# Norm weights multiplied into transposed q in place, and due times of single operations found by annealing, in an attention and feed-forward kernel on one core

## Chip, cores, metric

One core of one Trainium2 chip. The metric is the time of one execution on the device in microseconds (us), lower is better; medians over several executions.

## The reference, cut

Attention over q, k, v of shape (8, 12, 448, 64) with an RMS norm on q and k, then a feed-forward layer on the 3584 tokens of 768.

```python
def rmsnorm(x, g):
    return x / np.sqrt(np.mean(x * x, axis=-1, keepdims=True) + 1e-06) * g
q_n, k_n = rmsnorm(q, g_q), rmsnorm(k, g_k)
attn = softmax(q_n @ k_n.T / 8) @ v            # per batch and head
x = attn.transpose(0, 2, 1, 3).reshape(3584, 768)
h = x @ w_in                                    # 768 -> 2048
sp = np.maximum(h, 0.0) + np.log1p(np.exp(-np.abs(h)))
return (h * erf(sp)) @ w_out                    # 2048 -> 768
```

A "pair" below is two heads of one batch element; there are 48.

## The kernel before

The kernel adds some 3950 operations to a plan. Each has an engine (P TensorE, V VectorE, A ScalarE, G GpSimd, S SyncE), a cost in us and a due time. A list scheduler inside the kernel then walks through time and gives each free engine the ready operation with the earliest due time; what comes out is the order in which the instructions are emitted, so each engine runs them in that order on the chip. The plan also models a port that VectorE and GpSimd share: an operation marked `port` that finds the lock taken is lengthened until the lock's end.

```python
# Plan.order(), the part that starts an operation
took = o.cost if type(o.cost) is float else o.cost[e]
if e in "VG" and o.port:
    took += max(0.0, lock - now - 0.13)
    lock = now + took
free[e] = now + took
...
PAIR, BATCH, N_PE, N_COL = 8.59, 54.26, 8, 6
W_IN, W_OUT, W_RATE = 2, 9, 4
FILL, FILL_SHARE, MERGED, TWO_GROUPS = 1.98, 0.73, 1, 1
```

For a pair transposed by DMA, three GpSimd multiplications write a scaled copy of k (both norm weights in one vector `gcomb`) into one of two kp buffers, on a zero background, so that the third block of keys can be two full matmuls:

```python
for i, (r, c0, s0, w, c) in enumerate(((0, 0, S + D, JS, 0.75), (0, JS, S, D, 0.14), (D, S, S, S, 0.86))):
    ...
            nc.gpsimd.tensor_tensor(dst, src, g.to_broadcast((D, w)), op=ALU.mult)     # kp <- qT * gcomb
    add(engs, ..., t0 - 3, scaled, reads=["gcomb", ("qT", m), ("kp0", kp)], writes=[("kp", kp, i)], port=True)
```

The w_in loads are paced, one after each of the pairs 2 to 5:

```python
if 0 <= n - W_IN < NC:
    load = add_w_in(n - W_IN, [load, ends[-1]])
```

The softmax here doesn't subtract the row's maximum and nothing guards it: scores larger than these inputs give would overflow.

## Time and profile before

| | before |
|---|---|
| time, median of 3 | 475.87 us (475.81 to 478.84) |
| span of the profiled run | 473.3 us |
| busy: TensorE, VectorE, ScalarE, GpSimd | 448.1, 326.7, 376.1, 285.6 us |
| lost TensorE time 10 to 60, 60 to 180, 180 to end | 17.3, 15.5, 2.5 us |
| TensorE's own work | 424.0 us |

"Lost" is read as the prediction does: from the start of each matmul to the start of the next, less 189, 162.5 or 56 ns by its kind, where more than 0.11 us is left, and the whole of each idle product. (The prediction gives 2.7 us from 180 us on and 3.3 after the last matmul; counted again in the same way for all kernels, these are 2.5 and 3.7.) "Own work" is the span less what was lost, the time before the first matmul and the time after the last. All such figures, and the lags below, come from the one execution of each kernel that was profiled; executions of one kernel lie 1 to 7 us apart, so differences of 2 us or less between two of them say little. Three stages of the kernel before, by window (window and width, then busy us and instructions of PE, PEld, DVE, ACT, POOL, then clock, DMA share, GB/s):

```profile
100.00:120.00 20.00, 18.75 (x102) 8.71 (x100) 17.79 (x23) 15.05 (x24) 14.57 (x20) 1.00 0.55 93
180.00:240.00 60.00, 59.83 (x339) 30.57 (x338) 46.43 (x67) 52.91 (x72) 46.38 (x62) 1.00 0.59 144
300.00:320.00 20.00, 19.63 (x113) 10.80 (x111) 14.82 (x23) 19.26 (x20) 5.86 (x6) 1.00 0.28 86
```

After 180 us TensorE is all but full in every stage.

### The profile page before, as it was taken

To read this page: it belongs to the slowest core of one execution; us is meant where nothing else is said; L and a number is where in the kernel's file an instruction comes from. 1 tells how busy PE (TensorE), PEld (TensorE's weight loads), DVE (VectorE), ACT (ScalarE), POOL (GpSimd) and SP (SyncE) were. 2 spreads that over 40 slices of the span, in tenths; PEclk is the share of its full clock that TensorE was granted. 3 is DMA by queue.
4 is the path that set the end of the run, shared out by engine and by line. 5 is a ranking of instruction groups with operands and counts; after the bars stand their busy time and mean duration, and the time that the engine had idled before them with its cause. 6 is when DMAs were issued, how large, how long until landed. Compare 5 with 4: busy or idle time off the path is not lost.

```text
span 473.3 us, 7387 instructions
## 1 busy us (share of the span) xinstructions
PE 448.1 (95%) x2556; PEld 227.4 (48%) x2556; DVE 326.7 (69%) x460; ACT 376.1 (79%) x495; POOL 285.6 (60%) x393
## 2 busy tenths in 40 slices
PE   7768999899898999999999999999999999999997
PEld 3333344444344445554455445554455445655664
DVE  2986677698875997499866975598665933285811
ACT  3587887997789988997889988998889987996500
POOL 6898898858894599828992589619980560000000
PEclk9799999999999999999999999999999999999999
DMA  8929999875977056912793168704942111110221
GB/s 184 276 65 222 192 240 224 136 165 82 229 187 171 19 140 162 231 50 58 169 235 108 21 165 187 198 34 98 221 90 83 21 36 35 66 36 7 78 82 69
DMA packets 108646, 60.00 MB, mean 127 GB/s; under 512 B 59456, under 2 KB 108608, under 8 KB 108608
## 3 DMA queue, kind: packets, MB, share of 16 engines
q1 hardware_dynamic: 101824, 52.64, 46.3%
q0 software_dynamic: 5440, 6.29, 8.7%
q10 hardware_dynamic: 1344, 0.59, 0.5%
q8 instruction: 20, 0.33, 0.3%
q14 instruction: 18, 0.15, 0.1%
HBM read 45.61 MB, written 11.01 MB: 120 GB/s over the span
## 4 chain that ended last, share of the span: by engine, by line
PE 62%; POOL 14%; DVE 9%; ACT 6%; issue 5%; DMA 3%; SPq 1%; POOLq 0%; DVEq 0%; ACTq 0%
PE f L586 25%; PE f L536 21%; PE o L479 11%; POOL sq L265 5%; PE s L454 4%; POOL kp L305 3%; PE s L442 3%; DVE qk L283 2%; POOL qk L283 2%; DVE h L320 2%; POOL vx L413 2%; DMA sp<-in_k_dram 2%; ACT sp L554 1%; ACT sp L550 1%; POOL vm L408 1%
## 5 line engine op out<-in xcount | busy, mean ns | idle before, releaser
L536 PE MATMUL f<-xT,w_in_sb 128*128 128x448 bf16 x768 | 163.6, 353 | 4.9 <-DVE h L320 3.3
L460 ACT ACTIVATE e<-s 128x896 bf16<-128x896 f32 x144 | 126.3, 915 | 4.0 <-PE s L454 2.4
L305 POOL TENSOR_TENSOR kp<-qT,gcomb 64x384 bf16<-64x384 bf16 (+2 forms) x120 | 90.6, 761 | 61.6 <-PE s L454 57.0
L536 PEld LDWEIGHTS <-w_in_sb 128*128 128x128 bf16 x768 | 73.1, 98 | 81.2 <-issue 17.0
L320 DVE COPY h<-f 128x448 f32<-128x448 f32 x105 | 64.9, 620 | 31.3 <-PE f L536 30.2
L265 POOL TENSOR_TENSOR sq<-raw 128x896 f32<-128x896 f32 x42 | 72.6, 1729 | 18.7 <-DVE st L267 9.2
L479 PE MATMUL o<-e,vm 128*128 128x448 bf16 (+1 forms) x324 | 74.1, 360 | 3.7 <-DVE xT L501 1.4
L586 PE MATMUL f<-w_out_sb,g 128*128 128x384 bf16 x384 | 67.4, 326 | 0.8 <-DVE ob L320 0.8
L320 DVE COPY ob<-f 128x384 f32<-128x384 f32 x52 | 28.8, 556 | 55.3 <-PE f L586 54.0
L586 PE MATMUL f<-w_out_sb,godd 128*128 128x384 bf16 x384 | 65.1, 326 | 0.0
L267 DVE TENSOR_REDUCE st<-sq 128x14 f32<-128x896 f32 x42 | 45.5, 1084 | 20.1 <-POOL sq L265 19.5
L550 ACT ACTIVATE sp<-h 128x1792 f32<-128x1792 f32 x31 | 50.4, 1686 | 3.6 <-DVE h L320 3.5
L554 ACT ACTIVATE sp<-sp 128x1792 f32<-128x1792 f32 x32 | 52.6, 1690 | 0.1
L586 PEld LDWEIGHTS <-g 128*128 128x128 bf16 x384 | 37.0, 98 | 29.2 <-issue 4.6
L495 ACT ACTIVATE r<-o 64x448 f32<-64x448 f32 x42 | 22.7, 541 | 34.3 <-PE o L479 34.1
L586 PEld LDWEIGHTS <-godd 128*128 128x128 bf16 x384 | 37.3, 98 | 25.9 <-issue 1.1
L283 POOL TENSOR_TENSOR qk<-raw,st 128x512 bf16<-128x512 f32 x42 | 46.9, 1122 | 1.6 <-ACT st L272 0.3
L283 DVE TENSOR_TENSOR qk<-raw,st 128x384 bf16<-128x384 f32 x42 | 42.4, 1029 | 4.2 <-ACT st L272 2.6
L479 PEld LDWEIGHTS <-vm 128*128 128x128 bf16 (+1 forms) x324 | 28.0, 101 | 30.8 <-issue 8.5
L454 PE MATMUL s<-qT,kp 128*128 128x448 bf16 x120 | 35.7, 352 | 1.6 <-ACT e L460 1.5
L413 POOL CAST vx<-vs 64x64 bf16<-64x64 f32 x96 | 30.0, 314 | 7.1 <-PE o L479 2.7
L501 DVE TENSOR_TENSOR xT<-o,r 64x448 bf16<-64x448 f32 x42 | 25.7, 611 | 12.5 <-ACT r L499 12.0
(71 smaller groups left out, 483.3 us busy)
## 6 DMA issues: line engine op xcount, KB each, us to landing
vl<-in_v_dram SPq DMA_DIRECT2D x48, 192.0 KB, 3.6
out_dram<-ob SPq DMA_DIRECT2D x48, 192.0 KB, 1.9
raw<-in_q_dram SPq DMA_DIRECT2D x21, 384.0 KB, 4.4
raw<-in_k_dram SPq DMA_DIRECT2D x21, 384.0 KB, 4.9
w_in_sb<-in_moe_w_in_dram POOLq DMA_DIRECT2D x4, 768.0 KB, 9.2
w_out_sb<-in_moe_w_out_dram POOLq DMA_DIRECT2D x8, 384.0 KB, 5.1
vs<-in_v_dram SPq DMA_DIRECT2D x16, 96.0 KB, 4.9
out_dram<-ob SPq DMA_DIRECT2D x16, 96.0 KB, 2.2
```

What stands on the lines that cost most here:

```text
L265: add("G", 1.72, tg, lambda part=part: nc.gpsimd.tensor_tensor(sq, part, part, op=ALU.mult), reads=ks, writes=["sq"], port=True)
L267: add("V", 1.08, tg, lambda ss=ss, x=x: nc.vector.tensor_reduce(ss[:, 14 * x : 14 * x + 14], sq, axis=AX.X, op=ALU.add), reads=["sq"], wri ...
L283: add(eng, cost, tg - 27.29, lambda e=e, g=g: e.tensor_tensor(qks[qi].rearrange("p g h d -> p h g d")[:, :, g], raw[:, :, g], w[:, :, g, N ...
L305: nc.gpsimd.tensor_tensor(dst, src, g.to_broadcast((D, w)), op=ALU.mult)
L320: nc.vector.tensor_copy(dst, src)
L454: add("P", cost, t0 + s - 2.54, lambda dst=dst, lhs=lhs, rhs=rhs: nc.tensor.matmul(dst, lhs, rhs, start=True, stop=True), reads=[("qT", m) ...
L460: add("A", 0.918, t0 + s + 1.84, lambda e=e, st=st: nc.scalar.activation(e, st[:, :, :S], func=FN.Exp), reads=[("s", sl, 0), ("s", sl, 1), ...
L479: add("P", cost, t0 + s + 2.3, lambda s=s, dst=dst, lhs=lhs, rhs=rhs: nc.tensor.matmul(dst, lhs, rhs, start=(s == 0), stop=(s == 3)), read ...
L536: add("P", 0.1887, 1e4 + BATCH * (b + 1) + f, lambda f=f, kt=kt, fp=fp: nc.tensor.matmul(fp[:, :S], w_in_sb[:, kt, f * P : (f + 1) * P], x ...
L550: add("A", 1.665 + (1.283 if c == order[0] else 0), -1e3, lambda c=c, h=h: nc.scalar.activation(sps[c], h, func=FN.Softplus), reads=[("h", ...
L554: add("A", 1.665 + (1.283 if c == order[0] else 0), -1e3, lambda c=c: nc.scalar.activation(sps[c], sps[c], func=FN.Erf), writes=[("sp", c, ...
L586: add("P", 0.1617, 1e4 + BATCH * (b + 2.88) + ti, lambda src=src, col=col, nt=nt, js=js, fp=fp: nc.tensor.matmul(fp[:, :JS], src[nt // 4][ ...
```

## The change

Its intent: less work on GpSimd (one in-place multiplication of q by the norm weights and two small copies per pair, instead of three multiplications into kp), a start retuned with due times by batch, and a shorter plan, by due times of single operations found by annealing.

```diff
-    SEM = 0.08
+    SEM = 0.09
+DUES = {
+    0: -18.703, 1: -60.012, 2: -60.006, 4: -60.009, 5: 15.776, 6: -16.681, ...    # 1148 entries, cut
+}
-    N_VL, N_E, N_EM, N_R, N_X, N_H, N_O = 2, 4, 2, 2, 2, 5, 2
+    N_VL, N_E, N_EM, N_R, N_X, N_H, N_O = 2, 6, 2, 2, 2, 5, 2
-    kps = ring(sb, N_KP, [P, 7 * P], BF16, "kp")
+    kps = ring(sb, N_KP, [P, P], BF16, "kp")
-    PAIR, BATCH, N_PE, N_COL = 8.59, 54.26, 8, 6
-    W_IN, W_OUT, W_RATE = 2, 9, 4
+    PAIR, BATCH, N_PE, N_COL = 8.31, 54.15, 9, 6
+    W_IN, W_STEP, W_OUT, W_RATE = 1, 0, 7, 2
+    DUE = dict(...)                       # due offsets per kind and batch, cut
+    FILL, FILL_SHARE, MERGED = 1.19, 0.45, 1
-        for i, (r, c0, s0, w, c) in enumerate(...):       # three scaled copies into kp
+        def gained():
+            ...
+                nc.gpsimd.tensor_tensor(qT[:, :S], qT[:, :S], gcomb.to_broadcast((P, S)), op=ALU.mult)
+        add("G", {"G": 0.86, "V": 0.32}, t0 - DUE['sc'][b], gained, reads=["gcomb", ("qT", m)], writes=[("qTg", m)], port=True)
+        for i in range(2):
+            ...copied: kp[r, r] <- qT[r, S : S + D]
-                if split:
+                if split or s == 2:       # the third block is a pair of 64-row matmuls
-            if 0 <= n - W_IN < NC:
-                load = add_w_in(n - W_IN, [load, ends[-1]])
+            for c in range(NC):
+                if n == W_IN + c * W_STEP:
+                    load = add_w_in(c, [load, ends[-1]] if W_STEP or not c else [load])
+    for i, due in DUES.items():
+        plan.ops[i].due = due
     order = plan.order()
```

Also cut: row-tail loads in three pairs of transfers, copies out of PSUM on two engines in the first pair, the last block's copies in halves.

## The prediction

> **What bounds the kernel now.** I read the busy row of the page, its forty slices, the end of the chain, the stage table, the waits and the costliest groups, in that order.
>
> ```profile
> PE 448.1 (95%) x2556; PEld 227.4 (48%) x2556; DVE 326.7 (69%) x460; ACT 376.1 (79%) x495; POOL 285.6 (60%) x393
> ...
> PE   7768999899898999999999999999999999999997
> ...
> POOL 6898898858894599828992589619980560000000
> PEclk9799999999999999999999999999999999999999
> ```
>
> TensorE is the bound: 95% busy, at full clock apart from the first slices. Only the first third of the span has digits under 9 (and the last slice). But busy time flatters it, since a matmul's recorded span reaches into the next one. The rate at which matmuls really follow one another is in the last lines of the chain, in order of time (start us, us, what):
>
> ```profile
> 415.36 18.17 PE f L536 x96
> 433.53 36.41 PE f L586 x224
> 469.97 0.56 DVE ob L320
> ```
>
> 18.17/96 = 189 ns per 448-column matmul and 36.41/224 = 162.5 ns per 384-column one, though their rows give 353 and 326 ns. So I took the start of every matmul in the trace, subtracted these intervals (56 ns for the 128-column transposes), and call the rest above 0.11 us per gap, plus the idle products on the zero tile (189 ns each), lost:
>
> - 0 to 10.3 us: before the first real matmul, all lost.
> - 10 to 60 us: gaps 15.8 us, idle products 1.5: 17.3 us.
> - 60 to 180 us: gaps 10.8 us, 25 idle products 4.7: 15.5 us.
> - 180 to 470 us: 2.7 us in 290.
> - After the last matmul: 3.3 us.
>
> That is 49 us; 424 us of the 473 is matmul work at its own pace. The change can win only where time is lost. The stage table agrees (window, width, then busy us and instructions of PE, PEld, DVE, ACT, POOL, clock, DMA):
>
> ```profile
> 20.00:30.00 10.00, 8.13 (x66) 3.78 (x62) 7.59 (x12) 8.36 (x14) 9.62 (x11) 0.92 0.56 138
> 30.00:40.00 10.00, 7.53 (x71) 4.22 (x69) 9.37 (x11) 8.26 (x15) 9.53 (x9) 1.00 0.70 122
> 40.00:50.00 10.00, 7.59 (x55) 2.77 (x51) 4.32 (x9) 7.81 (x15) 7.83 (x14) 1.00 1.10 227
> ...
> 120.00:140.00 20.00, 17.13 (x99) 8.48 (x98) 15.56 (x16) 17.22 (x30) 19.12 (x27) 1.00 0.94 208
> 140.00:160.00 20.00, 18.40 (x100) 9.76 (x100) 14.65 (x23) 19.06 (x16) 8.86 (x9) 1.00 0.50 119
> ...
> 240.00:260.00 20.00, 20.00 (x118) 11.00 (x117) 13.30 (x20) 18.36 (x18) 11.44 (x12) 1.00 0.55 152
> ```
>
> From 20 to 40 us GpSimd is 95% busy, and in 120 to 140, where TensorE idles most after the start, 96%. The chain restricted to 115 to 150 us gives lines of GpSimd about 43% of that stretch. What GpSimd does (group line: busy us, mean ns; wait line: us in total, times, longest):
>
> ```profile
> L305 POOL TENSOR_TENSOR kp<-qT,gcomb 64x448 bf16<-64x448 bf16 x40 | 38.5, 962 | 2.7
> L305 POOL TENSOR_TENSOR kp<-qT,gcomb 64x384 bf16<-64x384 bf16 x40 | 35.0, 875 | 56.6 <-PE s L454 55.3 <-DMA qT<-qk 0.6
> L413 POOL CAST vx<-vs 64x64 bf16<-64x64 f32 x96 | 30.0, 314 | 7.1 <-PE o L479 2.7 <-DMA vs<-in_v_dram 1.5
> L305 POOL TENSOR_TENSOR kp<-qT,gcomb 64x64 bf16<-64x64 bf16 x40 | 17.8, 444 | 2.3 <-PE s L454 1.7
> ```
>
> ```profile
> POOL kp L305 <- PE s L454: 57.0, 10, 17.6
> ```
>
> Three multiplications per pair write a scaled copy of k into one of only two buffers, so GpSimd also stands 57 us waiting for score matmuls to free one. Most of that is late, where it costs nothing: the waits of 20 to 180 us hold 8.0 of it, in two pieces, one of 7.0 us.
>
> **What the Trainium skill says.** "Perfetto Trace Analysis", section "Identifying the Most-Contended Engine", says that matmul busy share does not show distance from the roofline; the trace agrees (353 ns recorded, 189 ns apart). "TensorEngine Tiling (Array Packing)", "Key Properties": changing the tiling mode drains TensorE. The trace agrees: near 190 us a group of two 64-row pairs has start-to-start times 285, 3, 197, 3, 282 ns, 0.58 us where two full matmuls would take 0.38. "GPSIMD Engine Reference", "4.1 Engine selection", says that two-input operations are about twice as slow there and one-input ones nearly line-rate; here the 64-column multiplication took 444 ns and the 64-column cast 314. "TensorE: Matmul & The Clock Gate", "What's actually happening", has the clock halved after an idle window of about 3.4 us; the trace has two such stretches, 11.3 to 14.7 and 18.1 to 21.5 us.
>
> **The change, part by part.**
>
> Norm weights. Per DMA-transposed pair, 0.962 + 0.875 + 0.444 = 2.28 us on GpSimd become one in-place multiplication of 128x448 and two 64x64 copies. The L305 rows give (962 - 875)/64 = 1.36 ns per column with no sign that partitions matter, so the multiplication should take about 0.96 us and the copies 0.31 as the casts: 1.59 us. The build has 39 such pairs (one more is transposed on TensorE): 40 x 2.28 - 39 x 1.59 = 29 us less on GpSimd, 286 to about 257. The path from the landed transpose to the first scores shrinks from three operations to one, 1.3 us, and the wait for a free kp goes, as the result stays in the four qT buffers.
>
> Scores. The third block can no longer be two full matmuls on zero-padded k; it becomes a 64-row pair. Alone that costs one entry and one exit: 285 + 3 + 282 - 189 = 381 ns, against 2 x 189 = 378. The build has 115 entries into 64-row mode against 64, yet nearly the same price: 39 x 0.003 us, plus a split pair and seven more transposes for the ninth TensorE-transposed pair, about +0.7 us in all.
>
> Start. The row-tail loads become three pairs of transfers instead of two, so pair 1 doesn't wait for 160 KB (now until 10.5 us); the first pair's two copies out of PSUM go to two engines at once instead of 0.38 + 0.44 us in line; six e buffers instead of four let the exponentials run ahead; all w_in loads follow pair 1. In the trace the first five attention results leave at 22.1, 27.8, 33.7, 38.5 and 42.6 us, 5.1 us apart, and the first projection matmul starts at 43.2. ScalarE needs 3 x 0.915 + 0.547 + 0.538 + 0.576 = 4.4 us per pair. At 4.5 us apart the fifth comes 2.5 us sooner; with some of the gaps up to 60 us closed as well I take 17.3 down to 12.5: -4.8.
>
> Order of single operations. The annealed due times move nearly everything between 40 and 180 us. The build holds 10 + 3 + 2 idle products in three places after the start, where before there were 25 in one; with the new share of 0.45 that is 15 x 0.19/0.45, about 6 us of gaps the schedule itself still expects, against 25 x 0.19/0.73 = 6.5. Unforeseen ones come on top (4 us seems fair, where about 9 of the 15.5 were unforeseen before), minus what less GpSimd work absorbs: 15.5 to 9: -6.5.
>
> After 180 us: 2.7 to 2.5, -0.2. End: the last block is copied by two engines in halves and stored from two queues, 0.56 us to about 0.33, and smaller stores: -0.5.
>
> Sum: -4.8 - 6.5 - 0.2 - 0.5 + 0.7 = -11.3, so 475.9 - 11.3 = 464.6 us; call it 464.5.
>
> **Rivals.** (1) GpSimd was never the cause: the gaps early on are a lack of matmul work, set by ScalarE's 4.4 us per pair and three table loads per batch. For it: ScalarE is 86 to 95% busy from 120 to 160, and DVE close behind. Against: GpSimd is busier in just the window with the longest gap. Then relief moves the wait to ScalarE and half of the middle gain goes: about 470. (2) Over-fitted order: each engine takes its instructions strictly in the planned order, so an order tight on paper loses when a load lands late; DMA already runs at a share above 1 in the stages 40 to 80 us, and all w_in loads now fall earlier. Against: from 180 us on the old plan lost 2.7 us in 290, so plans of this kind do hold. It would leave 468 to 474. (3) Everything closes, 10 to 180 us losing only about 12 of 33: about 455. (4) The mode changes cost more than the 3 ns when the pairs stand between other matmuls: 50 x 0.1 = +5 us, about 469.
>
> **Range and chances.** The threshold for 2% is 466.4, only 1.9 us above my number. Recovering a third of the 33 us lost between 10 and 180 gives 464; a quarter gives 467; half gives 459. As the change aims its whole effort at this loss I think better than a third somewhat likelier than worse: faster 0.61, same 0.37, slower 0.02; range 456.5 to 471.
>
> **What would show it.** Right: GpSimd busy near 257 us with the in-place row at 39 x about 0.96; no wait of GpSimd for score matmuls worth naming; the first projection matmul near 40.5 us; lost time about 12.5 in 10 to 60 and 9 in 60 to 180; TensorE's intervals still 189 and 162.5; span near 462. Wrong: the in-place row far above 1 us, gaps above 15 us again in 60 to 180 with ScalarE or DVE as releaser, a first projection matmul not before 43, or added time above 2 us at the 64-row pairs.

## The result

The changed kernel is slower: 491.25 us median of 4 runs (490.02 to 492.36) against 476.58 us for the kernel before on the same chip (475.81 to 478.84, 4 runs). The ratio is 1.0299, 95% interval 1.0254 to 1.0344. Here and below a ratio is the mean time of one kernel's fast runs over that of the other's of the same rounds, so not quite the ratio of the medians quoted. The output is correct.

The page of the changed kernel, busy row and TensorE's two rows of the forty slices:

```profile
PE 457.8 (93%) x2560; PEld 222.2 (45%) x2560; DVE 324.1 (66%) x463; ACT 379.2 (77%) x495; POOL 255.6 (52%) x388
...
PE   8488999878989999999999997999999999999996
...
PEclk9987999998989999999999999999999999999999
```

TensorE is busy for 10 us more and yet a smaller share of the span. In the row of before all slices from 160 us to the last but one were nines; here a 7 stands in the slice at 294 to 306 us. The clock row dips at four slices up to 150 us, where before it dipped at one. The stages from 20 to 50 us, and those of the table above:

```profile
20.00:30.00 10.00, 6.22 (x46) 2.73 (x44) 7.97 (x8) 5.95 (x12) 5.30 (x6) 0.83 0.49 122
30.00:40.00 10.00, 8.00 (x63) 3.36 (x61) 7.46 (x9) 8.68 (x17) 7.08 (x11) 1.00 0.78 148
40.00:50.00 10.00, 8.84 (x51) 3.26 (x51) 6.70 (x11) 6.36 (x12) 8.35 (x11) 0.66 0.74 152
100.00:120.00 20.00, 15.39 (x73) 6.33 (x72) 18.02 (x23) 13.91 (x19) 13.08 (x18) 0.91 0.53 94
180.00:240.00 60.00, 55.94 (x311) 26.93 (x310) 38.40 (x58) 50.76 (x68) 38.76 (x56) 1.00 0.57 141
300.00:320.00 20.00, 16.89 (x103) 9.47 (x101) 12.39 (x16) 14.78 (x14) 10.57 (x12) 1.00 0.54 138
```

Against the rows of before: 20 to 30 us fell from 8.13 to 6.22 busy us, 100 to 120 from 18.75 to 15.39, 180 to 240 from 59.83 to 55.94 and 300 to 320 from 19.63 to 16.89. From 30 to 50 us it is busier than before (8.00 for 7.53, 8.84 for 7.59), but at a clock of 0.66 in the second of these stages, where before it was 1.00. The span grew by 17.3 us, and the parts of the prediction's own table add up to that:

| us | before | predicted | after | change |
|---|---|---|---|---|
| before the first matmul | 10.3 | 10.3 | 10.6 | +0.3 |
| lost 10 to 60 | 17.3 | 12.5 | 20.3 | +3.0 |
| lost 60 to 180 | 15.5 | 9.0 | 17.9 | +2.4 |
| lost 180 to the last matmul | 2.5 | 2.5 | 10.0 | +7.5 |
| after the last matmul | 3.7 | 3.2 (-0.5) | 4.0 | +0.3 |
| TensorE's own work | 424.0 | 424.7 | 427.7 | +3.7 |

What the change does to GpSimd came out as intended. Groups (line, engine, operation, out<-in, count, busy us, mean ns, idle us before it and its releaser):

```profile
L499 POOL COPY kp<-qT 64x64 bf16<-64x64 bf16 x78 | 25.9, 333 | 54.1 <-PE s L664 51.1
...
L489 POOL TENSOR_TENSOR qT<-qT,gcomb 128x448 bf16<-128x448 bf16 x39 | 36.2, 930 | 19.1 <-DMA qT<-qk 18.7
```

The waits (engine, tile and line, what it waited for: us in total, times, longest):

```profile
POOL kp L499 <- PE s L664: 51.1, 8, 17.2
...
PE f L749 <- DVE h L513: 7.2, 5, 3.9
...
PE f L524 <- DVE g L582: 3.4, 1, 3.4
...
PE f L799 <- DMA w_out_sb<-in_moe_w_out_dram: 1.7, 1, 1.7
```

The in-place multiplication takes 930 ns, and GpSimd is busy 255.6 us. But its long wait for score matmuls did not go; it moved from the multiplications to the small copies. The other three lines are waits of TensorE. The longest, 3.9 us before 112 us, is for a VectorE copy behind a run of multiplications, the first of them at 102 us and over three times as long as the shortest of its line. The last is for a w_out load that had not landed, at 138 us. In between, the transposes wait, once and for 3.4 us, for a VectorE multiplication. That wait is read closely in the timeline (start us, us, engine, line, operation, out<-in, count, idle us before it and releaser):

```profile
18.23 0.95 POOL L604 CAST vm<-vl 128x384 bf16<-128x384 f32 x2
...
18.53 5.88 DVE L582 TENSOR_TENSOR g<-sp,s 128x896 bf16<-128x896 f32 x2 [0.64 <-DMA raw<-in_k_dram]
...
19.14 3.31 POOL L571 TENSOR_TENSOR sp<-sp 128x896 f32<-128x896 f32 x2
...
23.46 0.34 PE L524 MATMUL f<-ident,g 128*128 128x128 bf16 x3 [3.44 <-DVE g L582]
```

Two VectorE multiplications took 5.88 us, the first of them 4.88 where the shortest of that line takes 1.07. Meanwhile GpSimd ran four operations one after another, two casts and two multiplications, and TensorE stood 3.44 us until the product came. The same pattern at 301 us:

```profile
300.75 1.04 POOL L472 TENSOR_TENSOR qk<-raw,st 128x512 bf16<-128x512 f32 x1
...
301.17 3.68 DVE L472 TENSOR_TENSOR qk<-raw,st 128x384 bf16<-128x384 f32 x1
...
301.75 1.67 POOL L454 TENSOR_TENSOR sq<-raw 128x896 f32<-128x896 f32 x1
...
303.39 1.04 POOL L472 TENSOR_TENSOR qk<-raw,st 128x512 bf16<-128x512 f32 x1
...
305.43 0.73 PE L692 MATMUL o<-e,vm 128*128 128x448 bf16 x3 [2.46 <-DVE xT L714]
```

One VectorE multiplication (0.54 us at its shortest) took 3.68 us, beside three GpSimd operations without a gap between them; the VectorE operation that TensorE needed (xT, L714) came after it, and TensorE stood 2.46 us. In both cases the VectorE operation has two inputs in SBUF. Here the Trainium skill's page "SBUF — State Buffer", section "SBUF: two separate sides", bears on the case: VectorE with two SBUF inputs and GpSimd share a port pair as an exclusive lock, and the one that starts first has it for its whole instruction. The trace agrees that VectorE is held, but not that it is held for one instruction: it was passed over at the end of one GpSimd operation, and again at the next.

The kernel before has such cases too, this one at 124 us, in the stage whose idle TensorE the prediction put down to GpSimd's load:

```profile
123.83 2.03 POOL L305 TENSOR_TENSOR kp<-qT,gcomb 64x448 bf16<-64x448 bf16 x2
123.95 4.33 DVE L283 TENSOR_TENSOR qk<-raw,st 128x384 bf16<-128x384 f32 x2
...
125.83 2.04 POOL L283 TENSOR_TENSOR qk<-raw,st 128x512 bf16<-128x512 f32 x2
...
128.99 0.35 PE L479 MATMUL o<-e,vm 128*128 128x448 bf16 x1 [0.77 <-DVE xT L501]
```

Two VectorE multiplications took 4.33 us, the second of them 3.18, and soon after TensorE waited 0.77 us for a VectorE product that came behind it. Summed over the span, two-input VectorE operations lasted 31 us longer than the shortest of their line in the kernel before and 26 us in the changed one. So the holds did not become more. That each of them costs more in the changed kernel is what the experiments below test.

How it costs can be seen from the plan, since the kernel computes a start time for every operation. Take the real start of a matmul less its planned start as the lag. The old plan is 474.3 us long, and its last matmul starts 3.8 us earlier than planned: an early lag of 1.6 us is recovered. The new plan is 470.6 us long, 3.7 us shorter, and its lag climbs: +3.7 us after the held product at 19 us, +5.4 by 41 us, +8.5 after 112 us (another VectorE multiplication held 3.25 us at 102 us), +11.5 by 184, +16.4 after the one at 301 us, +16.7 at the end. Twice some of it is given back (from +6.7 to +3.1 between 97 and 106 us, from +11.3 to +9.3 between 155 and 163), and both times it is lost again within some 20 us; after 184 us no dip is over 1.2 us.

### The profile page after: what moved, and what is told of

The parts are those of the page before. It is cut to its first block, busy times and chain, and to the rows that moved or that the text cites. A ratio compares the mean times of both kernels' runs of the same rounds, so it can differ in the third digit from the quotient of the medians.

```text
span 490.6 us, 7353 instructions
## 1 busy us (share of the span) xinstructions
PE 457.8 (93%) x2560; PEld 222.2 (45%) x2560; DVE 324.1 (66%) x463; ACT 379.2 (77%) x495; POOL 255.6 (52%) x388
## 4 chain that ended last, share of the span: by engine, by line
PE 70%; DVE 8%; DMA 8%; POOL 5%; ACT 5%; issue 2%; SPq 1%; POOLq 0%; DVEq 0%
PE f L799 25%; PE f L749 24%; PE o L692 13%; PE s L664 5%; PE s L630 3%; DVE g L779 2%; DMA qT<-qk 2%; DVE qk L472 2%; DMA w_out_sb<-in_moe_w_out_dram 1%; DMA vl<-in_v_dram 1%; ACT sp L763 1%; POOL kp L499 1%; DMA sp<-in_q_dram 1%; ACT sp L767 1%; POOL sq L454 1%
## 5 line engine op out<-in xcount | busy, mean ns | idle before, releaser
L749 PE MATMUL f<-xT,w_in_sb 128*128 128x448 bf16 x768 | 166.6, 355 | 8.0 <-DVE h L513 7.2
L671 ACT ACTIVATE e<-s 128x896 bf16<-128x896 f32 x144 | 126.3, 915 | 17.7 <-PE s L664 10.7
L513 DVE COPY h<-f 128x448 f32<-128x448 f32 x116 | 71.2, 620 | 41.7 <-PE f L749 40.6
L692 PE MATMUL o<-e,vm 128*128 128x448 bf16 (+1 forms) x324 | 79.7, 366 | 4.5 <-DVE xT L714 2.5
L513 DVE COPY ob<-f 128x384 f32<-128x384 f32 x45 | 24.8, 555 | 54.3 <-PE f L799 50.3
L499 POOL COPY kp<-qT 64x64 bf16<-64x64 bf16 x78 | 25.9, 333 | 54.1 <-PE s L664 51.1
L472 POOL TENSOR_TENSOR qk<-raw,st 128x512 bf16<-128x512 f32 x42 | 49.4, 1179 | 8.2 <-ACT st L461 5.7
L489 POOL TENSOR_TENSOR qT<-qT,gcomb 128x448 bf16<-128x448 bf16 x39 | 36.2, 930 | 19.1 <-DMA qT<-qk 18.7
L472 DVE TENSOR_TENSOR qk<-raw,st 128x384 bf16<-128x384 f32 x42 | 35.7, 864 | 5.2 <-ACT st L461 2.7
L692 PE MATMUL o<-em,vx 128*128 128x448 bf16 (+1 forms) x108 | 34.0, 374 | 0.0
L664 PE MATMUL s<-qT 64*128 64x448 bf16 (+1 forms) x150 | 29.6, 376 | 3.7 <-ACT e L671 1.5
```

Of the source, the lines that this page charges most:

```text
L472: add(eng, cost, tg - DUE['nq'][b], lambda e=e, g=g: e.tensor_tensor(qks[qi].rearrange("p g h d -> p h g d")[:, :, g], raw[:, :, g], w[:, ...
L489: nc.gpsimd.tensor_tensor(qT[:, :S], qT[:, :S], gcomb.to_broadcast((P, S)), op=ALU.mult)
L513: nc.vector.tensor_copy(dst, src)
L664: add("P", cost, t0 + s - DUE['s'][b], lambda dst=dst, lhs=lhs, rhs=rhs: nc.tensor.matmul(dst, lhs, rhs, start=True, stop=True), reads=[(" ...
L671: add("A", 0.918, t0 + s + DUE['ae'][b], lambda e=e, st=st: nc.scalar.activation(e, st[:, :, :S], func=FN.Exp), reads=[("s", sl, 0), ("s", ...
L692: add("P", cost, t0 + s + DUE['aa'][b], lambda s=s, dst=dst, lhs=lhs, rhs=rhs: nc.tensor.matmul(dst, lhs, rhs, start=(s == 0), stop=(s == 3)),
```

## The experiments

Theory: the annealed order is too tight. It assumes that VectorE waits for one GpSimd operation and that loads land as planned; where that fails, the delay is on the path and stays. Rivals: the in-place multiplication itself or its 64-row pairs cost the time; the retuned parameters do; or the lower clock (17.1 us at half clock against 6.8) is a cause of its own. "The time before" in each case is that of the runs beside it, 476.9 to 478.2 us.

### The table of due times taken out

```diff
-    for i, due in DUES.items():
-        plan.ops[i].due = due
```

> The changed kernel without the annealed due times of single operations; everything else of the change stays. Theory A (the annealed order has no slack, so that each late operation delays all that follows): most of the 15 us goes, 475 to 481 us, and lost TensorE time after the start falls from 49 us to 33 or less. Theory B (the in-place weights and their 64-row pairs cost it): stays at 487 us or more. Between, both have a share.

Measured: 484.45 us, ratio 1.0142 (1.0105 to 1.0178). The lag of the end is +1.9 us. Its plan is 6.7 us longer than the one with the table, yet it is about 7 us faster. So the table itself makes about half of the loss, and the rest of the change makes the other half; the time lies between the two theories' ranges, as "both have a share" has it.

### The in-place multiplication alone, on the kernel before

```diff
-    three scaled copies into kp (448, 384 and 64 columns), due t0 - 3        # abridged
+    nc.gpsimd.tensor_tensor(qT[:, :S], qT[:, :S], gcomb.to_broadcast((P, S)), op=ALU.mult)
+    two copies kp[r, r] <- qT[r, S : S + D]; all three due t0 - 20.53
-                if split:
+                if split or s == 2:
```

The due times are the old ones but for these three operations: they have the changed kernel's, 17.5 us ahead of the old.

> The kernel before with the norm weights in place alone (one multiplication, two 64x64 copies, third score block as a 64-row pair), its old due times and parameters. Theory B: 485 us or more. Theory A: within 1% of 476.6, 474 to 481; TensorE's own work up by 1 to 3 us for 40 more entries into 64-row mode, GpSimd busy 27 us less.

Measured: 480.64 us, ratio 1.0072 (1.0036 to 1.0108). The busy row of its page, and its wait for score matmuls:

```profile
PE 449.8 (95%) x2560; PEld 220.8 (46%) x2560; DVE 314.1 (66%) x456; ACT 377.6 (79%) x499; POOL 254.2 (53%) x391
```

```profile
POOL kp L308 <- PE s L455: 63.1, 14, 17.1
```

GpSimd fell from 285.6 to 254.2 us, and TensorE's busy time rose by 1.7 us. Lost time is 18.2 us in 10 to 60, 15.5 in 60 to 180 and 4.5 after that, against 17.3, 15.5 and 2.5 before (the profiled execution is the fastest of this kernel, 477.97 us). Taking 31 us of work off GpSimd closed none of the gaps. But the relief did not reach the stages in which the prediction found GpSimd full, as the stage table of this run shows:

```profile
20.00:30.00 10.00, 8.13 (x68) 3.67 (x64) 7.65 (x12) 8.29 (x14) 9.52 (x11) 0.95 0.57 139
30.00:40.00 10.00, 7.68 (x59) 3.81 (x55) 9.56 (x11) 7.25 (x14) 9.36 (x9) 0.83 0.70 119
120.00:140.00 20.00, 16.84 (x99) 7.84 (x98) 12.56 (x19) 17.62 (x30) 18.62 (x32) 1.00 0.92 217
```

GpSimd is busy 9.52, 9.36 and 18.62 us there, where before it was 9.62, 9.53 and 19.12. So this run can't say whether its load in these stages makes the gaps. The wait for score matmuls went up from 57.0 to 63.1 us. TensorE's own work is 424.5 us, +0.5, with 103 entries into 64-row mode against 64, so the prediction's near-equal price of a pair and two full matmuls holds in this order.

### The planned order of VectorE and GpSimd made binding

66 GpSimd operations wait for the VectorE operation that the plan starts ahead of them; the order is untouched.

```diff
+    # for each VectorE operation on the port: the next GpSimd operation of the plan waits for it
+        for d in held.get(o, ()):
+            tc.add_manual_dep(o.inst.ins, d.inst.ins.name, must, reason="VectorE first")
```

> The changed kernel, same order on every engine, but 66 GpSimd operations wait for the VectorE operation that the plan puts before them, so that VectorE is not held behind a run of GpSimd operations on their shared port. Theory A with holds as the late events: the three long holds (3.8, 2.3 and 3.2 us) go and with them about 10 us, 479 to 484 us. If the holds are only a symptom: 489 to 493. If the added waits cost more than they save: above 493.

Measured: 483.94 us, ratio 1.0135 (1.0103 to 1.0167), 7 us less than the changed kernel. More waits made it faster. The place at 18 us, in the same view as before:

```profile
18.51 3.06 DVE L582 TENSOR_TENSOR g<-sp,s 128x896 bf16<-128x896 f32 x2 [0.64 <-ACT s L578]
18.67 0.95 POOL L604 CAST vm<-vl 128x384 bf16<-128x384 f32 x2
...
20.63 0.56 PE L524 MATMUL f<-ident,g 128*128 128x128 bf16 x7 [0.16 <-DVE g L582]
20.65 4.10 POOL L571 TENSOR_TENSOR sp<-sp 128x896 f32<-128x896 f32 x2 [1.03 <-DVE g L582]
```

The two VectorE multiplications take 3.06 us in place of 5.88, GpSimd's multiplications start after them, and TensorE waits 0.16 us instead of 3.44. The lag of the end is +7.0 us in place of +16.7. What is left comes in steps at 33 to 38 us (+2.4), 101 to 108 (+2.2), 168 (+2) and 226 to 230 (+1.5), less two dips. The step at 168 us is a price of the binding itself: a small copy that now waits for VectorE comes late, and TensorE stands 1.9 us for it.

### Only the first hold removed

```diff
-            if nxt is not None and nxt.start < v_.end + 0.5:
+            if v_.idx in (86, 87) and nxt is not None:
```

> The changed kernel with only the first long hold taken away: the GpSimd squares of pairs 4 and 5 wait for VectorE's multiplications of pairs 2 and 3. If what is lost once is never recovered in this order (Theory A): 3 to 4 us less, 487.5 us. If the order has slack that takes it up later: within 1 us of 491.

Measured: 488.44 us, ratio 1.0235 (1.0203 to 1.0268), 2.8 us less than the changed kernel, for a TensorE wait of 3.44 us taken away at 19 us. Some 470 us later most of that is still there: a delay in this order is not recovered. The hold of the multiplication at 301 us appears again, with 3.67 us at 295 us, so it belongs to the order and is no accident of one run.

### The same binding on the kernel before

> The kernel before, same planned order, but 66 GpSimd operations wait for the VectorE operation that the plan started ahead of them, as in the run of the changed kernel with the planned port order made binding (which gained 7 us there). Theory (held VectorE operations hurt only where the order has no slack; before runs 3.8 us faster than its own plan in the end): within 1% of before, 474 to 480 us. Rival (holds cost every kernel of this family about the same): 7 us less, about 470 us, which would also beat both kernels.

The edit is that of the third experiment. Measured: 479.96 us, ratio 1.0033 (0.9995 to 1.0070). Holds there cost nothing that binding wins back. The rival, that they cost every kernel of the family the same, falls.

### Twice the share of idle products

```diff
-    FILL, FILL_SHARE, MERGED = 1.19, 0.45, 1
+    FILL, FILL_SHARE, MERGED = 1.19, 0.9, 1
```

> The changed kernel with twice the share of idle products in planned gaps (0.9 for 0.45), nothing else. Rival (the lower granted clock, 17.1 us at half clock for 6.8 before, is a cause of its own and not a consequence of the gaps): half clock falls to 10 us or less and the time by 3 us or more, to 488 or less. Theory (the gaps that let the clock fall are not in the plan, so idle products placed by the plan miss them): half clock stays above 13 us and the time within 1% of the changed kernel, 489 to 493 us.

Measured: 490.26 us, ratio 1.0263 (1.0207 to 1.0319). Time at half clock fell from 17.1 to 6.8 us, which the theory had not expected, but the time fell by no more than the spread. In the changed kernel 25 matmuls ran at half pace and cost 4.5 us (8 and 1.4 us before), an upper bound of some 3 us for the clock as a cause; taking most of that away gave 1 us at best.

### Binding without the table

> The changed kernel without the table of annealed due times, plus the planned port order made binding for 64 GpSimd operations. Theory (the annealed order left no slack for held operations, the unannealed one did): the gain is much smaller than the 7 us of the annealed order, 0 to 3 us against the kernel without the table, so 481 to 485 us. Rival (both costs are independent and add up): 477 us, level with before.

Both edits together. Measured: 481.82 us, ratio 1.0083 (1.0047 to 1.0120): 2.6 us less than without the binding, against 7 us with the table. The tight order needs the binding more, and with the port bound in both the table costs only some 2 us (483.94 against 481.82, a difference hardly outside the intervals). From 45 us on its matmuls stay within 1.5 us of the plan; the last has a lag of -0.9 us.

### The w_in loads paced as before, without the table

```diff
-    W_IN, W_STEP, W_OUT, W_RATE = 1, 0, 7, 2
+    W_IN, W_STEP, W_OUT, W_RATE = 2, 1, 7, 2
```

> The changed kernel without the table, with the w_in loads paced as before (one after each of pairs 2 to 7 instead of all six after pair 1); the rest of the retuning stays. Its own plan is 3.6 us longer (481.0 for 477.3). If the early w_in loads are what delays the v load at 31 us (6.2 us landing for 3.6 planned), the step of the lag between 31 and 37 us (2.6 us) goes, and the time against the kernel without the table changes by -2.6 plus up to 3.6, that is 482 to 486 us, with lost TensorE time in 10 to 60 us under 14. Rival (the loads have nothing to do with it): the step stays and the time is 486 to 489 us.

(The loads are four, not six as that text has it, and follow pairs 2 to 5.)

Measured: 480.73 us, ratio 1.0075 (1.0021 to 1.0129), 3.7 us less than with the early loads, although its plan is 3.6 us longer. In the loads of 28 to 38 us (source, engine, count, KB each, median us to landing) the v load of a pair took, in the changed kernel and then with the pacing:

```profile
vl<-in_v_dram SPq DMA_DIRECT2D x2, 192.0 KB, 6.8
```

Without the table and with early loads it was 4.8 us. With the pacing:

```profile
vl<-in_v_dram SPq DMA_DIRECT2D x3, 192.0 KB, 3.0
```

GpSimd's wait for it between 25 and 45 us, without the table and then with the pacing:

```profile
POOL vm L604 <- DMA vl<-in_v_dram: 3.2, 1, 3.2
```

```profile
POOL vm L604 <- DMA vl<-in_v_dram: 0.2, 1, 0.2
```

And the stage 30 to 40 us of the two, in the columns of the stage table:

```profile
30.00:40.00 10.00, 6.36 (x49) 2.62 (x48) 7.68 (x11) 6.30 (x13) 6.76 (x7) 0.92 0.60 127
```

```profile
30.00:40.00 10.00, 8.02 (x70) 3.30 (x66) 9.08 (x11) 8.73 (x16) 9.81 (x12) 1.00 0.89 166
```

The step of the lag at 31 to 37 us is gone (the lag is -1.0 there) and 8.02 us of TensorE time stand where 6.36 did. Lost time in 10 to 60 us is 12.7 us in place of 15.9. As the plan orders everything after a changed load anew, the later stages differ as well (60 to 180 us: 20.1 for 19.4; after 180: 5.3 for 7.6); the early part of the gain is the load, the later part may be the new order.

### A new order, annealed with the port bound

If a tight order only needs its assumption to be made true, annealing on the in-place kernel and then binding the port should pay. A new table was annealed with the plan's own rules (a fifth of the score was the length of the same order under late loads).

> The in-place norm weights alone on the kernel before (480.6 us in its own run), with due times of single operations annealed anew on the kernel's own plan (now 467.8 us long, was 476.9; a fifth of the annealing's score is the length of the same order under late loads), and with 73 GpSimd operations made to wait for the VectorE operation that the plan starts ahead of them. So far the time was the plan's length plus the lag of the end plus 5.3 us, and the lag was -3.8 (before), -3.7 (in place alone), -0.9 (held, without the table), +16.7 (changed kernel), +7.0 (changed kernel, held). Theory (a tight order pays if what it assumes of the port is made binding and the loads are paced as before): lag -3 to +2, so 470 to 475 us, 0.6 to 1.7% under before. Rival (any order annealed on the length loses on the chip, whatever is bound): lag over +7, 480 us or more.

> The same new order, but nothing made to wait beyond what the data need. Theory: the order loses where VectorE is held past more than one GpSimd operation, 3 to 8 us more than the kernel with the same order held, so 474 to 481 us. Rival (the waits do nothing for an order with paced loads): the same time within 1 us.

Measured: with the port bound 482.62 us, ratio 1.0118 (1.0080 to 1.0156); not bound 494.74 us, ratio 1.0348 (1.0312 to 1.0384). The binding is worth 11 us here, so the cost of the port is shown again, on an order that I made. But the theory as stated falls: the plan is 9.1 us shorter than that of its parent, and the kernel is 2 us slower (480.64 for the parent). The lag of the end is +8.7. The page:

```profile
PE 458.8 (96%) x2546; PEld 220.2 (46%) x2546; DVE 305.3 (64%) x452; ACT 382.3 (80%) x503; POOL 247.4 (52%) x391
```

TensorE is 96% busy, more than in the kernel before, and the kernel is slower. The lost time in 10 to 180 us did fall, from 33.7 to 25.4 us. What grew is TensorE's own work, from 424.5 to 434.5 us. Its mode (number of active rows and columns) changes 269 times, in the parent 209 times: the annealing had pulled 64-row matmuls apart. A matmul ahead of a change to 64 rows takes 285 ns to the next start, one ahead of its like 189, so 60 more changes are worth some 5.8 of these 10 us. The plan has one flat price for a pair, wherever it stands.

### The same for the changed kernel with paced loads

> The changed kernel with w_in loads paced as before, its due times annealed anew (plan 469.6 us, was 481.0) and 68 GpSimd operations held. Its parent without table and holds had a lag of -5.6. Theory: lag -4 to +2, time 471 to 477 us. Rival (retuning of the rest of the changed kernel costs on the chip what no plan shows): 480 us or more.

Measured: 486.88 us, ratio 1.0202 (1.0182 to 1.0222). Mode changes: 320, against 224 without the table; TensorE's own work 441.2 us against 425.9, of which 96 changes at 96 ns are worth 9.2. The rival's number came in, for a reason that I had not named.

### Annealing with mode changes priced

```diff
+                if e == "P":
+                    took, mode = took + 0.095 * (o.mode != mode), o.mode
```

Every small matmul costs 0.1 us in this plan. Port bound, new tables.

> The kernel before with its own operations and parameters, due times annealed anew on a plan that prices TensorE by its modes (0.095 us at each change, 0.1 us for a small matmul, instead of flat prices), plan 469.4 us long, and 68 GpSimd operations held behind the VectorE operation planned ahead of them. Theory (the annealed orders lost because these two prices were wrong): lag of the end -3 to +3 us, so 472 to 478 us by plan plus lag plus 5.3, TensorE's own work not over 426 us. Rival (an order annealed on length is brittle whatever is corrected, as small deviations anywhere are on the path): lag over +6, 481 us or more, with gaps spread over the span.

> The changed kernel with w_in loads paced as before and its table annealed anew on the plan priced by modes (465.7 us long), 64 GpSimd operations held. Theory: lag -3 to +4, 468 to 475 us, level with or better than before; mode changes well under the 320 of the order annealed without that price. Rival: lag over +8, 479 us or more.

Measured: on the kernel before 483.61 us, ratio 1.0130 (1.0074 to 1.0186), own work 428.8 us, lag +10.7; on the changed kernel with paced loads 477.93 us, ratio 1.0016 (0.9959 to 1.0074), 243 mode changes, own work 428.5 us, lag +7.8. So the changed kernel, with paced loads, bound port and mode changes priced, is level with the kernel before, 13 us under the changed kernel as it was. Here the annealed table paid: the next experiment is the same kernel bound and paced but without a table, and takes 481.72 us. It doesn't beat the kernel before, and on that kernel annealing again made a good kernel worse: there the rival came in, with its lag over +6 and its time over 481 us. Two repaired prices are not all.

### Both repairs without a table

> The changed kernel without its table, with w_in loads paced as before and the planned port order made binding. Apart, the two were worth 3.7 and 2.6 us against the kernel without the table (484.5). Theory (costs add): 478 us, level with before. Rival (the two remove the same waits): 480 to 481 us.

Measured: 481.72 us, ratio 1.0116 (1.0052 to 1.0181). Binding adds nothing to paced loads in an order that was not annealed; the rival's number came in, 1 us over.

## Why the prediction was wrong

The loss splits along a ladder of kernels, each with one more part (all ratios to before):

| kernel | ratio | step |
|---|---|---|
| before, with the in-place multiplication | 1.0072 | +0.0072, 3.4 us |
| and the rest of the retuning, loads paced as before | 1.0075 | +0.0003 |
| and the early w_in loads | 1.0142 | +0.0067, 3.2 us |
| and the table: the changed kernel | 1.0299 | +0.0157, 7.5 us |

(us: the step times 477. Each ratio has an interval of about 0.004 to either side, so the first and third steps are each about as sure as two such intervals allow; the last is clear.) And the lags of the end, with the length of the plan:

| kernel | plan, us | lag of the last matmul, us | time, us |
|---|---|---|---|
| before | 474.3 | -3.8 | 476.6 |
| in place alone | 476.9 | -3.7 | 480.6 |
| changed, no table | 477.3 | +1.9 | 484.5 |
| changed, no table, paced | 481.0 | -5.6 | 480.7 |
| changed | 470.6 | +16.7 | 491.3 |
| changed, port bound | 470.6 | +7.0 | 483.9 |
| in place, new order, bound | 467.8 | +8.7 | 482.6 |
| paced, new order, bound | 469.6 | +13.9 | 486.9 |
| before, priced order, bound | 469.4 | +10.7 | 483.6 |
| paced, priced order, bound | 465.7 | +7.8 | 477.9 |

Every annealed order has a lag of 7 us or more; no other has more than 1.9 (the kernels left out of the table fit: +12.4 and +13.6 for two more runs of the changed kernel's table, -0.9 to +1.7 for the rest). A lag alone doesn't decide: the last row lags by 7.8 us on a plan 15 us shorter than that of the same kernel without a table, and is faster than it.

**What bounds the kernel.** Right that TensorE does. That the busiest neighbour, GpSimd at 96% in 120 to 140 us, causes the gaps was read from its busy share, and stays unproven: with 31 us of its work gone (in place alone) lost time was no less, but in just these stages GpSimd stayed as full. In that stretch a held VectorE operation stands in the trace, yet binding the port gained nothing in this kernel. Rival (1), that ScalarE sets the early gaps, was not tested either. Rival (3), that everything closes, fell with the lost time.

**Norm weights.** Sizes right: 255.6 us for 257, 930 ns for 960, copies 333 ns for 314. Wrong that the wait for score matmuls goes: it moved to the copies, 51.1 us after 57.0, as they still write one of two kp buffers. It is mostly late, and no run here shows a cost of it.

**Scores.** +0.7 us predicted, +3.7 measured. In place alone has +0.5, as worked out. The retuning without the table has +2.3, the table the rest, as it splits groups of 64-row matmuls (227 mode changes become 237). Rival (4) has this size of cost but not this reason.

**Start.** -4.8 predicted, +3.0 measured. The parts of the start that were counted may have worked: without the table and with paced loads lost time was 12.7 us, the 12.5 predicted. Two things not counted took it: the early w_in loads, which I listed as a help and which delay the v load (15.9 us with them, no table), and the hold at 18.5 us (20.3 us in the changed kernel, 17.4 with this hold removed). The first projection matmul came at 54.3 us and not at 40.5; the new plan itself has it at 48.8.

**Order of single operations, the step that failed.** -6.5 predicted for 60 to 180 and -0.2 after that; +2.4 and +7.5 measured. Two things in it failed. The first is the reading of the plan. The working took the plan's gaps from its 15 idle products, 6 us, and added 4 us for the unforeseen. But the kernel puts idle products only into planned gaps above 1.19 us. The plan, run again from the kernel's source, has these gaps on TensorE (those above 0.11 us), beside what the chip lost:

| us | before: plan, chip | changed: plan, predicted, chip | changed, no table: plan, chip |
|---|---|---|---|
| 10 to 60 | 9.9, 17.3 | 6.5, 12.5, 20.3 | 6.1, 15.9 |
| 60 to 180 | 16.4, 15.5 | 14.0, 9.0, 17.9 | 16.2, 19.4 |
| after 180 | 6.2, 2.5 | 5.5, 2.5, 10.0 | 10.6, 7.6 |

So from 60 to 180 us the new plan itself had 14.0 us of gaps and not 6; the 4 us for the unforeseen came out right. By its length it claimed a gain of 3.7 us, where 11.3 were predicted.

The second is the trust that the plan holds on the chip. From 180 us on the old plan did better than it said (2.5 us lost for 6.2), the new one worse (10.0 for 5.5), and its start is 14 us worse than planned. Against the same kernel without it, the table adds 4.4 us at the start, 2.4 after 180 us and 1.3 of own work, and saves 1.5 in between: what is lost more from 60 to 180 us is there without the table.

Rival (2), the over-fitted order, names what happened, and was set aside because "from 180 us on the old plan lost 2.7 us in 290, so plans of this kind do hold". That compared unlike things. The old plan comes from a few parameters and had slack that nobody counted, the 3.7 us above; the new one was picked out of very many by the plan's own price list, and so, as I read it, also for what the list has wrong. The runs show two such places: the port, where VectorE is passed over (7 us by binding it), and in the new orders of mine the mode changes. Rival (2) also named the late load, which is the third. Its range, 468 to 474 us, was too mild: it let the order keep part of the gain.

**Still open.** When VectorE gets the port after one GpSimd operation and when it is passed over: both are seen in the traces, and no rule came out of them. Why the priced orders still lag by 8 and 11 us. Why the in-place multiplication alone costs 3.4 us: 0.5 is own work, and in the profiled execution 0.9 more is lost at the start and 2.0 after 180 us. Why the retuning loses more from 60 to 180 us, with or without early loads. Why the retuned kernel has 1.8 us more of TensorE's own work than the in-place one when neither has a table; part of it is seven more transposes.

## What to carry to other kernels

An order searched on the length of a model's plan must be judged on the chip, by that length and its lag together: of the five annealed orders here four lost more in lag than they had gained in length, and the fifth gained only after the port was bound and the mode changes priced. The runs fit the view that such a search finds the model's wrong prices first and uses up the slack that would have taken them in. When a prediction rests on a plan that the kernel computes, run the plan and read its gaps; its idle products show only the long ones. Before relieving a busy engine, look in the trace for the operation that the idle one waits for, and whether the relief reaches that stage. A VectorE operation three times as long as its like was here held, not slow. When the order of VectorE and GpSimd on their shared port matters, it can be made binding with a dependency; here 66 added waits made a tight kernel 7 us faster and did nothing for one with slack.

## What the Trainium skill lacked or had wrong

- "SBUF — State Buffer", on the shared port of VectorE and GpSimd: it gives the pair to the one that starts first and has the other blocked while that instruction runs. These runs show a VectorE multiplication held past the ends of several GpSimd operations in a row: 4.88 us beside four of them, 3.25 us beside two multiplications and the start of a cast, 3.68 us beside three, for operations of 1.07, 0.94 and 0.54 us. In the last case it had started 0.58 us before the second of the three. In other cases VectorE came in after the first (1.23 us, at 124 us); the page has no rule for being passed over, and neither have the runs.
- "TensorEngine Tiling (Array Packing)", "Key Properties": it says that a change of tiling mode drains TensorE and gives no price there. In the kernel before, the matmul ahead of a change from full to 64 rows took 285 ns to the next start in place of 189, so about 0.1 us for a change; 60 and 96 more changes came with 10 and 15 us more of TensorE's own work.
